# Gated mix of sliding-window attention and a gated feed-forward network: the last 1024 tokens' down projection as seven products of block sums, transposed

## The chip, the core and the metric

The kernel runs on one core of a Trainium2 chip, in one launch. Its engines are PE (TensorE, matrix products into PSUM), DVE (VectorE), ACT (ScalarE), POOL (GpSimd) and SP (SyncE, which issues most DMAs). Each engine works through its own instructions in order; they wait for each other by semaphores. The metric is the device time of one execution in microseconds (us).

## The reference

```python
x = A_x                                        # 2048 tokens x 512
g = sigmoid((x * gate_w).sum(-1, keepdims=True))
q, k, v = heads(x @ wqkv)                      # 32 heads of 16
s = q @ k.T * 16 ** -0.5                       # key i - 255 .. i for query i
a = (softmax(s) @ v) @ wo
b = (silu(x @ w_gate) * (x @ w_up)) @ w_down   # 512 -> 1792 -> 512
return g * a + (1 - g) * b
```

All of it is fp32.

## The kernel before, in words

**Precision.** An fp32 product is made of three matmuls on operands that are split into a high part (a cast to fp32r, on ACT) and a low part (a subtraction, on DVE or POOL): high x high, high x low, low x high. `split` makes the parts (lines 67 and 70), `mm3` issues the three matmuls (L85 to L87). A matmul has 128 rows of depth and 512 moving columns; 12 of them make one *step* of a down projection: one hidden tile of 128 rows, one chunk of 512 tokens, four blocks of 128 tokens.

**Tiles.** The 2048 tokens are four chunks (c = 0 to 3) of 512; the 1792 hidden columns are 14 tiles of 128; the 32 heads are eight groups of four.

**First part, to 598 us.** After a start of about 85 us (values, first projections) come eight groups of 16 slots. A slot (some 4.1 us) is written out by hand in program order: for each of its four heads two score products (L275, L314), their maximum (DVE, L277) and exponential (ACT, L316), three pairs of matmuls of a *lane* (L225: the gate and up products of the hidden tiles 0 to 12 and the q/k projections, into PSUM buffers `pa` and `pb`), and whatever the table `AT` holds for this slot and head (`later(t, hd, f)`). Once in four slots `av` (L338) multiplies the exponentials with the values, and `finish` (L353 to L368) takes its result out of PSUM in five pieces: a copy on ACT, an addition and a copy on DVE (L355, L357), a transpose, the division, a transpose back and the store to `od`. The gate and up products go to DRAM (`raws`, L525). Waiting weights are fetched one ahead into one buffer `raw` (L75), whose low half POOL makes. Before a group begins, its q and k rows are copied into place by SP (`stack`, L258 and L259) out of a pair of buffers `xhi`, `xlo` (`x_pair`). In the last slots `tile0` (L588, L589) makes the hidden tile 0 of chunk 0 and its two halves `TILE0`.

**Tail, from 598 us.** For each chunk 14 steps. Hidden tile `ORDER[n]` is loaded from `raws` (L689, two loads of 256 KB into the pool `got`, four buffers each), goes through SiLU (ACT, L703) and a product (DVE, L704), is split (L67, L70) and is multiplied with the split down weights (`step`). Tile 13 (the second of `ORDER`) has its gate and up products made here, 24 matmuls a chunk (L700). The attention's output projection (`attn_out`, 12 matmuls for each of the 16 token blocks) lies between the steps of chunks 1 to 3. The two results are weighted and added (`put`, L675), and `out` is stored in blocks of 128 tokens. `last_steps` does the last two steps block by block, so that each block's end (L745) runs beside the next block's matmuls; its last block's last step is done in two halves of 256 columns.

## Time and profile before

| | us |
|---|---|
| median of 3 runs (lowest, highest) | 821.86 (821.36, 822.3) |
| span of the profiled execution | 821.5 |
| DVE busy | 515.6 |
| ACT busy | 448.9 |
| POOL busy | 351.8 |

The page lists no time of the profiled execution beside its span, so the span stands for it. A row of a timeline reads: start, length, engine, line, operation, output from inputs, shape, count, and in brackets the idle time ahead of it with what ended it. A row of the windows has busy time and instruction count of PE, PE's weight loads, DVE, ACT and POOL, then clock, DMA share and GB/s. The clock granted to TensorE is 1.000 over the span, and 133.26 MB are moved by DMA.

### The profile page before, as it was taken

To read this page: it belongs to the slowest core of one execution; us is meant where nothing else is said; L and a number is where in the kernel's file an instruction comes from. 1 tells how busy PE (TensorE), PEld (TensorE's weight loads), DVE (VectorE), ACT (ScalarE), POOL (GpSimd) and SP (SyncE) were. 2 spreads that over 40 slices of the span, in tenths; PEclk is the share of its full clock that TensorE was granted. 3 is DMA by queue.
4 is the path that set the end of the run, shared out by engine and by line. 5 is a ranking of instruction groups with operands and counts; after the bars stand their busy time and mean duration, and the time that the engine had idled before them with its cause. 6 is when DMAs were issued, how large, how long until landed. Compare 5 with 4: busy or idle time off the path is not lost.

```text
span 821.5 us, 21573 instructions
## 1 busy us (share of the span) xinstructions
PE 815.1 (99%) x8329; PEld 683.8 (83%) x8329; DVE 515.6 (63%) x1437; ACT 448.9 (55%) x936; POOL 351.8 (43%) x640
## 2 busy tenths in 40 slices
PE   8999999999999999999999999999999999999998
PEld 7888988888888888888888888888887888888886
DVE  6397677677667676677677667756567453443543
ACT  6422666666656666666666666656654433333341
POOL 7812555555546555645554655456511221011020
PEclk9999999999999999999999999999999999999999
DMA  8574534624534543552562463466698563383531
GB/s 294 164 206 150 154 121 125 191 94 146 166 128 125 161 146 117 152 170 101 144 193 102 126 191 125 160 207 201 210 325 267 182 197 110 131 244 107 178 125 51
DMA packets 67957, 133.26 MB, mean 162 GB/s; under 512 B 11600, under 2 KB 16336, under 8 KB 67856
## 3 DMA queue, kind: packets, MB, share of 16 engines
q1 hardware_dynamic: 63888, 118.00, 46.3%
q0 software_dynamic: 3968, 13.90, 4.6%
q8 instruction: 65, 1.06, 0.6%
q14 instruction: 36, 0.29, 0.1%
HBM read 61.08 MB, written 45.61 MB: 130 GB/s over the span
## 4 chain that ended last, share of the span: by engine, by line
PE 95%; DMA 2%; DVE 1%; ACT 1%; issue 1%; SPq 0%; DVEq 0%; ACTq 0%
PE pb L225 24%; PE pa L225 24%; PE pb L338 7%; PE ps L275 6%; PE ps L87 5%; PE ps L85 5%; PE ps L86 5%; PE ps L314 5%; PE pb L205 2%; PE pa L205 2%; PE pb L85 2%; PE pb L87 2%; PE pb L86 2%; PE ps L338 2%; DMA got<-raws 1%; PE pb L700 1%
## 5 line engine op out<-in xcount | busy, mean ns | idle before, releaser
L277 DVE CUSTOM_DVE_ANT_0 ps<-ps,mask 128x384 f32<-128x384 f32 (+2 forms) x512 | 271.6, 539 | 143.2 <-PE ps L314 66.7
L316 ACT ACTIVATE pt<-ps 128x384 f32<-128x384 f32 (+2 forms) x512 | 240.7, 477 | 114.9 <-PE ps L275 57.7
L318 POOL TENSOR_SCALAR_AFFINE_SELECT pt<-pt 128x256 f32<-128x256 f32 x256 | 107.4, 419 | 223.8 <-ACT pt L316 220.4
L314 PE MATMUL ps<-q,k 64*128 64x384 f32 (+2 forms) x512 | 159.9, 329 | 0.0
L275 PE MATMUL ps<-k,q 63*128 63x384 f32 (+2 forms) x512 | 158.7, 330 | 0.0
L225 PE MATMUL pb<-xhi,wh 64*128 64x512 f32 x512 | 111.3, 394 | 0.0
L225 PE MATMUL pb<-xlo,wh 64*128 64x512 f32 x512 | 110.1, 391 | 0.0
L225 PE MATMUL pb<-xhi,wl 64*128 64x512 f32 x512 | 109.9, 392 | 0.0
L225 PE MATMUL pa<-xhi,wh 64*128 64x512 f32 x512 | 109.0, 394 | 0.0
L225 PE MATMUL pa<-xhi,wl 64*128 64x512 f32 x512 | 107.9, 391 | 0.0
L225 PE MATMUL pa<-xlo,wh 64*128 64x512 f32 x512 | 107.8, 391 | 0.0
L275 PEld LDWEIGHTS ps<-k,q 63*128 63x128 f32 x512 | 88.8, 185 | 16.9 <-issue 5.7
L321 POOL TENSOR_SCALAR_AFFINE_SELECT pt<-pt 128x256 f32<-128x256 f32 x224 | 98.7, 441 | 0.0
L314 PEld LDWEIGHTS ps<-q,k 64*128 64x128 f32 x512 | 89.9, 184 | 5.4 <-issue 0.8
L704 DVE TENSOR_TENSOR sg<-got,sg 128x512 f32<-128x512 f32 x51 | 45.1, 885 | 64.6 <-ACT sg L703 59.9
L338 PE MATMUL ps<-pt,vg 64*32 64x320 f32 (+4 forms) x1408 | 75.0, 346 | 0.0
L338 PE MATMUL pb<-pt,vg 64*32 64x320 f32 (+3 forms) x1360 | 73.9, 350 | 0.0
L277 DVE DVE_READ_ACCUMULATOR2_ANT mx<- 128x1 f32 x512 | 71.9, 140 | 0.0
L338 PEld LDWEIGHTS pb<-pt,vg 64*32 64x32 f32 x1360 | 46.4, 106 | 28.3 <-ACT pt L316 9.9
L225 PEld LDWEIGHTS pb<-xhi,wh 64*128 64x128 f32 x512 | 56.6, 185 | 7.9 <-ACT ev L522 0.3
L225 PEld LDWEIGHTS pb<-xhi,wl 64*128 64x128 f32 x512 | 56.5, 184 | 6.7
L225 PEld LDWEIGHTS pa<-xhi,wl 64*128 64x128 f32 x512 | 54.7, 184 | 7.4
(159 smaller groups left out, 1576.6 us busy)
## 6 DMA issues: line engine op xcount, KB each, us to landing
raws<-ev SPq DMA_DIRECT2D x104, 256.0 KB
got<-raws SPq DMA_DIRECT2D x102, 256.0 KB
od<-o POOLq DMA_DIRECT2D x32, 256.0 KB, 2.6
raw<-wgu SPq DMA_DIRECT2D x28, 256.0 KB
q<-xhi SPq DMA_DIRECT2D x56, 128.0 KB
k<-xhi SPq DMA_DIRECT2D x56, 128.0 KB
vd<-vs POOLq DMA_DIRECT2D x8, 672.0 KB, 5.1
vg<-vd SPq DMA_DIRECT2D x32, 168.0 KB
```

The lines of the kernel that those rows point to most:

```text
L85: nc.tensor.matmul(ps, lh, rh, start=start and i == 0, stop=False, skip_group_check=skip)
L86: nc.tensor.matmul(ps, lh, rl, start=False, stop=False, skip_group_check=skip)
L87: nc.tensor.matmul(ps, ll, rh, start=False, stop=stop and i == n - 1, skip_group_check=skip)
L225: mm = nc.tensor.matmul(ps[me], w[r], x[r], start=not second and i == 0, stop=bool(second) and i == n - 1)
L275: nc.tensor.matmul(ps[:, :n], QT[g % 2][pr][r, q0:q0 + P], KT[g % 2][pr][r, k0:k0 + n], start=True, stop=True)
L277: mx = nc.vector.tensor_tensor_reduce(out=ps[:, :n], in0=ps[:, :n], in1=mask[:, 3 * P - n:], scale=1.0, scalar=NEG, op0=ALU.add, op1=ALU.m ...
L314: nc.tensor.matmul(ps[:, :n], KT[g % 2][pr][r, k0:k0 + P], QT[g % 2][pr][r, k0:k0 + n], start=True, stop=True)
L316: BEHIND.append(nc.scalar.activation(pt[:, j, :n], ps[:, :n], AF.Exp, scale=SCALE))
L318: nc.gpsimd.affine_select(out=pt[:, :, :P], in_=pt[:, :, :P], pattern=[[0, 2], [1, P]], compare_op=ALU.is_ge, fill=0.0, base=0, channel_mu ...
L321: nc.gpsimd.affine_select(out=pt[:, :, 2 * P:], in_=pt[:, :, 2 * P:], pattern=[[0, 2], [-1, P]], compare_op=ALU.is_ge, fill=0.0, base=-1, ...
L338: nc.tensor.matmul(AV[g, c][h][32 * j:32 * j + 32, q0 - c * CH:q1 - c * CH], VG[4 * g + kb // 4][o, kb % 4, 17 * j:17 * j + 32], PT[g, kb, ...
L704: nc.vector.tensor_tensor(out=sg, in0=gu[1], in1=sg, op=ALU.mult)
```

## The change

Let H be the hidden activations of the last 1024 tokens, cut into 2 x 2 blocks: tokens of chunk 2 or 3, hidden tiles 0 to 6 or 7 to 13. The down weights are cut into 2 x 2 blocks as well: tiles 0 to 6 or 7 to 13, output columns 0 to 255 or 256 to 511. The product of two such matrices needs eight block products; with sums and differences of blocks as operands seven do (a scheme of Strassen and Winograd). Each is 7 tiles x 2 column blocks x 3 matmuls. They are made transposed: weights stand still, 512 tokens move.

- *Sums of weights* (`sums`, new): 14 sets, two in each of the first seven groups, each for one pair of weight tiles and half their columns. At slot 16g+3 or 16g+6 two loads of 128 KB into `xhi`; one slot later, at head 2, four additions of 128x128 on DVE (L593); one more slot later a split, and two stores of 256 KB to `sd`.
- *`raws`* keeps gate and up of a tile and chunk side by side, so that one load of 512 KB takes both. `ORDER` pairs tile k with tile k + 7.
- *Gates* of chunks 2 and 3 go to DRAM and come back spread over all partitions, since in a transposed result the gate varies along the columns.
- *Tail, first part:* the step of `TILE0` comes first, then the last tile's products of all four chunks (`last_tile`, 96 matmuls), then the remaining steps of chunks 0 and 1, with the attention output of these chunks as 8 steps among them ("a"), then the attention output of chunks 2 and 3, transposed, as 8 steps ("T"). Beside them the 26 loaded activations of chunks 2 and 3 are made (`ready`) and held, and their block sums formed (`first_sum`, `third_sum`, `operand`). `got` has four buffers of 512 KB, which all of these share with the stored weight sums.
- *Tail, last part:* 49 steps of 6 matmuls in the order of products 1, 5, 6, 2, 7, 3, 4 (`block`), with the operands three steps ahead (`LEAD`); the results of a product are put together and weighted by `after` and `finished`, two pieces a step, and stored to a second output `outT`.
- The tail's splits are by ACT and DVE; POOL has none.

The core of the diff:

```diff
-    raws = dram.tile([NF - 1, 2, NCH, P, CH], F32, name="raws")
+    raws = dram.tile([NF - 1, NCH, P, 2, CH], F32, name="raws")
+    sd = dram.tile([4, P, NP, 2, HD], F32, name="sd")
-    ORDER = [0, NF - 1, *range(1, NF - 1)]
+    ORDER = [0, NF - 1, 7, 1, 8, 2, 9, 3, 10, 4, 11, 5, 12, 6]
...
+        def sums(t, k, d):
+            u = slice(d * P, d * P + P)
+            buf = []
+            def load():
+                buf.extend(x_pair())
+                uv = buf[0][:, :CH].bitcast(F32).rearrange("p (r c) -> p r c", c=P)
+                for m in range(2):
+                    nc.sync.dma_start(uv[:, 2 * m:2 * m + 2], wd[k + NP * m].rearrange("p (r c) -> p r c", r=2)[:, :, u])
+            def add():
+                parts = buf[0].bitcast(F32).rearrange("p (r c) -> p r c", c=P)
+                a11, a21, a12, a22, *to = (parts[:, r] for r in range(8))
+                for n, (x, y, op) in enumerate(((a21, a22, ALU.add), (to[0], a11, ALU.subtract),
+                                                (a11, a21, ALU.subtract), (a12, to[1], ALU.subtract))):
+                    nc.vector.tensor_tensor(out=to[n], in0=x, in1=y, op=op)
...
+            later(t, 1, load)
+            later(t + 1, 2, add)
+            later(t + 2, 0, halve)
+            later(t + 2, 3, store)
+        for m in range(2 * NP):
+            sums(m // 2 * NB + 3 + m % 2 * 3, *divmod(m, 2))
...
-        hp = B.enter_context(tc.tile_pool(name="hp", bufs=3, side="right"))
+        hp = B.enter_context(tc.tile_pool(name="hp", bufs=4, side="right"))
...
+        HALF["h", 0, 0] = TILE0
+        multiply(("h", 0, 0))
+        source(plan[0][0])
+        last_tile(0)
...
+        last_tile(3)
+        gates()
...
+        def operand(p, k):
+            if p == 6:
+                sub(T1[k], R[k + NP, 3], T1[k])
+            if p == 4:
+                sub(T1[k], R[k + NP, 2], T1[k])
...
+        def block(p, k, ds=range(2), cols=slice(0, CH)):
+            hh, hl = HALF[p, k]
+            for d in ds:
+                mm3(bank(p)[d][:, cols], [(block_weights(p, k, d), (hh[:, cols], hl[:, cols]))],
+                    start=p in (1, 5, 2, 3) and k == 0, stop=k == NP - 1, skip=True)
...
+        x = BANK["pa"]
+        for d in range(2):
+            for cols in ((slice(0, CH),), (slice(0, CH // 2), slice(CH // 2, CH)))[d]:
+                for p, k in steps[end:]:
+                    block(p, k, (d,), cols)
+                for f in finished(2, 2 + d, x[d], cols=cols):
+                    f()
```

The lines of the changed kernel are 4 higher than those of before in the attention part (L277 is L281, L225 is L229, L355 is L359, L357 is L361), and 2 higher in `split` and `mm3` (L70 is L72, L85 to L87 are L87 to L89).

**Order on DVE in an attention slot.** DVE in slot 16g+4 at head 2, where `finish` takes a result out of PSUM. An ISA row pair is a score block's maximum; `o` is the result, `pb` the PSUM buffer. Before:

```order
L277 ISA ps_8680,mx<-ps_8680,mask 128x384
L277 ISA mx 128x1
L355 TENSOR_TENSOR o_1341<-pb,o_1341 128x448
L357 COPY o_1341<-pb 128x64
L277 ISA ps_8698,mx<-ps_8698,mask 128x384
```

The changed kernel:

```order
L281 ISA ps_8830,mx<-ps_8830,mask 128x384
L281 ISA mx 128x1
L593 TENSOR_TENSOR xhi<-xhi 128x128 x4
L359 TENSOR_TENSOR o_1347<-pb,o_1347 128x448
L361 COPY o_1347<-pb 128x64
L281 ISA ps_8852,mx<-ps_8852,mask 128x384
```

The four additions stand between the maximum and the pair that empties `pb`.

**Order on PE at the start of the tail.** The last value product (L338, now L342) and what follows it. Before:

```order
L338 MATMUL ps_10569<-pt,vg 32x128
L700 MATMUL pa<-xhi_71,wh 128x512
L700 MATMUL pa<-xlo_72,wh 128x512
L700 MATMUL pa<-xhi_71,wl 128x512
```

The changed kernel (`k_363` holds TILE0's halves, `q_90` the down weights):

```order
L342 MATMUL ps_10745<-pt,vg 32x128
L87 MATMUL ps_10837<-q_90,k_363 128x512
L88 MATMUL ps_10837<-q_90,k_363 128x512
L89 MATMUL ps_10837<-q_90,k_363 128x512
L87 MATMUL ps_10838<-q_90,k_363 128x512
```

The 12 matmuls of the first step moved ahead of the last tile's gate and up products.

**Order on PE and DVE at the end.** PE's last step and a half, in the changed kernel, with the engines that a row waits for; `pa` is the last result (128 output columns by 512 tokens, halves of 256):

```order
L89 MATMUL pa<-hh,k_362 128x256
L87 MATMUL pa<-hh,q_90 128x256
L88 MATMUL pa<-hl,q_90 128x256
L89 MATMUL pa<-hh,q_90 128x256
L87 MATMUL pa<-hh,q_361 128x256 [waits DVE_49]
L88 MATMUL pa<-hl,q_361 128x256
```

And DVE's last rows there (L72 is a low half, L835 a difference of operands, L963, L966, L969 the addition, gate product and last addition of a result):

```order
L835 TENSOR_TENSOR xhi_11480<-h_10976,xhi_11480 128x512
L72 TENSOR_TENSOR hl<-xhi_11480,hh 128x512
L963 TENSOR_TENSOR sg<-ps_12453,woh 128x512
L966 TENSOR_TENSOR sg<-sg,xlo_11016 128x512
L72 TENSOR_TENSOR hl<-xhi_11480,hh 128x512
L969 TENSOR_TENSOR sg<-sg,raw_12026 128x512
L963 TENSOR_TENSOR sg<-ps_12454,woh 128x512
L966 TENSOR_TENSOR sg<-sg,xlo_11016 128x512
L969 TENSOR_TENSOR sg<-sg,raw_12027 128x512
L966 TENSOR_TENSOR sg<-pa,xlo_11016 128x512
L969 TENSOR_TENSOR sg<-sg,k_11949 128x512
L966 TENSOR_TENSOR sg<-pa,xlo_11016 128x256
```

Where before four results followed their matmuls one by one at the end, the last operand's low half now stands among the results of another product, and PE's last nine matmuls stand behind the gate product of the first half of their own PSUM tile.

401 lines of the change are left out of this document (285 added, 116 removed).

## The prediction

> **What bounds the kernel now.** I read the page first, its busy times and its chain, then the waits of the matmul engine, then the timeline at the places that the change touches.
>
> ```profile
> span 821.5 us, 21573 instructions
> PE 815.1 (99%) x8329; PEld 683.8 (83%) x8329; DVE 515.6 (63%) x1437; ACT 448.9 (55%) x936; POOL 351.8 (43%) x640
> PE 95%; DMA 2%; DVE 1%; ACT 1%; issue 1%; SPq 0%; DVEq 0%; ACTq 0%
> ...
> PE pa L180 <- POOL ident masks.py:199: 1.4, 1, 1.4
> PE ps L87 <- DVE hl L70: 0.4, 1, 0.4
> ```
>
> PE (TensorE's matmuls) is busy 99% of the span and makes 95% of the chain, and its list of waits (last two rows: microseconds in total, times, longest) is nearly empty. So each matmul removed pays its full pace, and each wait that appears on PE costs its full length: no idle time on PE is left to take it. The first thing needed is that pace, from the chain:
>
> ```profile
> 640.86 2.72 PE pa L700 x12
> 643.58 2.72 PE pb L700 x12
> ```
>
> Twelve matmuls of 512 columns take 2.72 us, 0.2267 us each.
>
> **The removed matmuls: -9.5 us.** The down projection of chunks 2 and 3 was 2 x 14 steps of 12 matmuls, 336. It becomes 7 products x 7 tiles x 6, 294. The attention output of these chunks is only transposed and keeps its count, and so does the last gate/up tile. 42 x 0.2267 = 9.52 us. The rows of PE fall from 6758 to 6722 in the order, 36 and not 42, because nine matmuls, not three, now stand as two halves (6 more rows, 0.07 us). The rest of this part asks where PE must now wait.
>
> **The first step of the tail: +2.9 us.** The tail began with 24 gate/up products (L700) that need nothing new. Now chunk 0's first down step (operand TILE0) stands there.
>
> ```profile
> 598.11 1.28 ACT L588 ACT_TABLE_LOAD   x1
> 599.40 0.63 ACT L588 ACTIVATE ev<-k 128x512 f32<-128x512 f32 x1
> 600.07 0.69 DVE L589 TENSOR_TENSOR ev<-k,ev 128x512 f32<-128x512 f32 x1 [4.59 <-ACT ev L588]
> 600.79 0.62 ACT L67 CAST k<-ev 128x512 fp32r<-128x512 f32 x1 [0.76 <-DVE ev L589]
> 601.45 0.69 DVE L70 TENSOR_TENSOR k<-ev,k 128x512 fp32r<-128x512 f32 x1 [0.69 <-ACT k L67]
> 598.87 0.50 PE L700 MATMUL pa<-xhi,wh 128*128 128x512 f32 x1
> ...
> 604.22 0.39 PE L700 MATMUL pb<-xhi,wl 128*128 128x512 f32 x1
> ```
>
> The five rows of ACT (ScalarE) and DVE (VectorE) are one dependent chain that the change leaves alone. It ends at 601.45 + 0.69 = 602.14. PE is free at 598.87; the step's first two matmuls need the cast (601.41), the third the subtraction. It starts near 602.2 where it could have stood at 598.87 + 0.45: 2.9 us, formerly covered by the L700 products. I see no cover now; bounds 2.5 to 3.2.
>
> **The sums in the attention slots: +4.5 us.** 14 times, two DMA loads, four DVE additions of 128x128, a cast, a subtraction and two stores are put into the slots, some 0.9 + 0.6 us of DVE each. DVE has 37% of its time free, so only the place counts. The additions stand in order (first excerpt above) ahead of the L355/L357 pair that empties a PSUM buffer. In the group of 355 us:
>
> ```profile
> 359.06 0.57 DVE L277 CUSTOM_DVE_ANT_0 ps<-ps,mask 128x384 f32<-128x384 f32 x1 [2.33 <-PE ps L314]
> 359.55 0.14 DVE L277 DVE_READ_ACCUMULATOR2_ANT mx<- 128x1 f32 x1
> 359.55 0.62 DVE L355 TENSOR_TENSOR o<-pb,o 128x448 f32<-128x448 f32 x1
> 360.08 0.22 DVE L357 COPY o<-pb 128x64 f32<-128x64 f32 x1
> 360.21 0.56 DVE L277 CUSTOM_DVE_ANT_0 ps<-ps,mask 128x384 f32<-128x384 f32 x1
> 360.43 0.33 PE L314 MATMUL ps<-q,k 64*128 64x384 f32 x1
> ...
> 360.60 0.41 PE L225 MATMUL pb<-xhi,wh 64*128 64x512 f32 x2
> 98.92 0.21 DVE L357 COPY o<-pb 128x64 f32<-128x64 f32 x1
> 99.14 0.55 PE L225 MATMUL pb<-xhi,wh 64*128 64x512 f32 x2
> ```
>
> The L225 product on `pb` takes the buffer that L357 empties at 360.30, so it has 0.30 us to spare; in the first group (98.92 + 0.21 against 99.14) it has none. From 64 columns to 448 the start-to-start time of such operations goes from 0.13 to 0.53 us in these rows (360.08 to 360.21, 359.55 to 360.08), which gives about 0.20 us for 128; with two dependent hand-overs the four take about 0.9 us. PE then waits 0.9 - 0.3 = 0.6 us in six groups and 0.9 in the first: 4.5 us. No row shows a 128x128 addition. The lower bound is 0.5 us (the next L277 can slip and PE reaches `pb` later than shown); the upper is four durations of 0.29, the 128-column row of L277 below, or 1.16 us, giving 6 x 0.86 + 1.16 = 6.3.
>
> ```profile
> L277 DVE CUSTOM_DVE_ANT_0 ps<-ps,mask 128x128 f32<-128x128 f32 x32 | 9.2, 294 | 32.8 <-PE ps L275 24.4 <-POOL x10lo L70 6.1 <-PE ps L314 2.3
> ```
>
> The Trainium skill, "VectorE: DVE Perf Modes", section on the TRN2 errata, puts an fp32 tensor_tensor at (N+151)/0.96 ns and says that small tiles pay the fixed part each time; for 512 it gives 0.69, as L589 above shows. By it an addition is 0.29 us, and four in a row would make the upper 6.3 us; the overlap of consecutive rows above (0.62 long, the next 0.53 later) speaks for less. The second set of a group stands three slots later, by the same rows at a place with no pair to empty: 0 to 0.1 us each, in the bounds.
>
> The additions also wait for their loads, and DVE works in order: a late load holds all behind it.
>
> ```profile
> 350.85 0.60 SPq L259 DMA_DIRECT2D k<-xhi  x1
> ...
> 353.71 1.13 SPq L525 DMA_DIRECT2D raws<-ev  x2
> 362.76 0.33 SPq L75 DMA_DIRECT2D raw<-wgu  x1
> 370.19 0.14 DVE L277 DVE_READ_ACCUMULATOR2_ANT mx<- 128x1 f32 x1
> od<-o POOLq DMA_DIRECT2D x32, 256.0 KB, 2.6
> ```
>
> SP (the queue that issues) reaches the first pair of loads after 353.71, behind the last copy out of the same buffer (issued 350.85). With 1 us of issue and the 2.6 us of the only 256 KB transfer that the page times, it lands near 358.6, before 359.55. The second pair comes behind the wait that ends at 362.76, five issues of about 0.5 us and its own slot, and lands near 369; the additions follow the row of 370.19 there. Both are close, and the same SP also carries the attention's own loads.
>
> **The tail's loads: +1.5 us.** The first of them must wait for all stores of the attention output, the last of which is issued at 605.28:
>
> ```profile
> 605.28 0.56 POOL L368 DMA_DIRECT2D od<-o  x1 [5.83 <-DVE o L367]
> ```
>
> With 2.6 us to land and 3 to load, data come near 612. The 96 products of the last tile, 21.8 us, now stand ahead of the first step that needs them and hide this. Then loads of 512 KB replace pairs of 256 KB, and the tiles of chunks 2 and 3 come earlier: while the remaining steps of chunks 0 and 1 run, 20 steps or 54.4 us ask for 35 loads and 1 MB of stores or other loads, 19.4 MB, 357 GB/s. What such loads got:
>
> ```profile
> 600.00:610.00 10.00, 10.00 (x46) 8.28 (x45) 7.45 (x13) 5.49 (x11) 0.56 (x1) 1.00 0.95 333
> 610.00:620.00 10.00, 10.00 (x46) 8.29 (x45) 9.76 (x18) 2.98 (x5) 0.00 (x0) 1.00 0.92 313
> 620.00:630.00 10.00, 9.64 (x42) 7.40 (x41) 7.71 (x10) 5.81 (x10) 2.78 (x2) 1.00 0.89 292
> ```
>
> (Last columns: clock, DMA share, GB/s.) At 333 the 19.4 MB take 58.3 us, 3.9 too many, which three spare buffers of the four (1.5 MB, 4.7 us) about cover. At 292 they take 66.4 us, 12 too many, 7 uncovered. I take 1.5, near the best row, since the 292 was not asked for more; bounds 0 and 7. The Trainium skill, "DMA: Bandwidth & Descriptors", section Specifications, states about 358 GB/s of HBM per core; by it the stage would just fit and this term would be 0. The rows stay below that at a share of 0.95, so the measured rates decide.
>
> **The end: +5.0 us.** Before, four L745 operations follow their matmuls on an idle DVE:
>
> ```profile
> 817.40 0.28 PE L87 MATMUL ps<-k,hl 128*128 128x256 f32 x1
> 817.72 0.88 DVE L745 SCALAR_TENSOR_TENSOR k<-ps,igate,k 128x256 f32<-128x256 f32 x2 [0.64 <-PE ps L87]
> ```
>
> Last matmul to end of span is 821.5 - 817.68 = 3.8 us, 2.9 of it behind DVE (818.60). Now each operand of the last product is a subtraction, a cast and a subtraction, and DVE also does the results of products 7 and 3. From the first operand of product 4 to the last low half stand 21 DVE operations in order, 21 x 0.60 (512 columns by the two start-to-start times above), with hand-overs between dependent ones and the last cast about 14.0 us. PE needs it at 8 steps x 1.36 + 8 x 0.2267 = 12.7: **1.3 late**. Behind that half DVE still has four operations of product 3, two of product 4's first column block, and the first 256-wide one, about 4.4 us; and the matmuls of the last 256 columns wait for that one (third excerpt), where they could have followed after 1.5: **3.0**. After them stand a multiplication and an addition in place of one operation, 0.44 more, and some 0.3 of hand-over: **0.7**. The 3.0 is order alone; if the operands are in time the sum is 3. If DVE runs as in this row (885 ns against 600), it reaches 8.
>
> ```profile
> L704 DVE TENSOR_TENSOR sg<-got,sg 128x512 f32<-128x512 f32 x51 | 45.1, 885 | 64.6 <-ACT sg L703 59.9 <-DMA got<-raws 4.7
> ```
>
> **Sum.** 821.5 - 9.5 + 2.9 + 4.5 + 1.5 + 5.0 = 825.9 in the profiled execution, which lies 0.4 below the median of the runs (821.86): **826**.
>
> **Rivals.**
> - *The additions fit and the loads come in time.* DVE's free 37% speaks for it, the in-order rows above against. Attention 0.5, loads 0, end 3.0: 821.5 - 9.5 + 2.9 + 0.5 + 3.0 = 818.4, with the median 818.7, faster.
> - *One of the two large terms fails.* Attention hidden, the end as computed: 821.5 - 9.5 + 2.9 + 0.5 + 1.5 + 5.0 = 821.9, with the median 822.2, no difference.
> - *The loads bound the middle of the tail*, as soon as they get under about 310 GB/s over those 54 us; the rows of 313 and 292 speak for it, that these were not asked for more against it. 7 in place of 1.5: 831.7, slower.
> - *The second pair of loads in each group is late* by 0.7 us, which holds DVE and then PE in six groups: +4.2, about 830.4. This decides as soon as the landing passes 370.2.
> - That the matmuls do not go away is excluded by the order; what can fail is only that PE uses the time.
>
> **How the numbers follow.** A measurement of this kernel tells 0.2% (1.6 us) from no change, so faster is under 820.2 and slower over 823.5. The forecast has 0.46 (0.06 of it in its lower flank, within 0.2%), the first rival 0.29, the second 0.09, the loads 0.10, the late pair 0.06. Faster 0.29, same 0.06 + 0.09 = 0.15, slower 0.40 + 0.10 + 0.06 = 0.56. The range leaves out the far halves of the first rival and of the load-bound case: 817 to 832. The forecast's own range is 823 to 829.
>
> **What would show it.** Right: a wait of PE of 2 to 3 us just before its first down step at 599; waits of 0.6 on `pb` behind the copy of the attention pair, seven times; two gaps on PE in its last 20 us, the larger ahead of its last nine matmuls; under 1.5 us of waits in between. Wrong: no PE wait on DVE in the attention slots (the first rival), additions that idle for their DMA (the late pair), or a row of PE waits in steps 12 to 31 that end with DMA (loads). The prediction fails as a whole if PE's listed waits add up to under 8 us.

## The result, and the profile after

| | before | changed |
|---|---|---|
| median of the runs beside each other (lowest, highest), us | 822.08 (821.36, 823.23) | 851.16 (850.42, 854.79) |
| span of the profiled execution, us | 821.5 | 849.8 |
| granted clock over the span | 1.000 | 0.987 |

The changed kernel is slower: ratio 1.036, 95% interval 1.0336 to 1.0384. The prediction was 826.0 (817 to 832). The sign was right and the size was not. In the experiments below one run of `r_end`, 899.05 us at a granted clock of 0.85, is left out as slow.

The head of the changed kernel's page (busy times, the granted clock in 40 slices, the chain by engine):

```profile
span 849.8 us, 21755 instructions
PE 822.3 (97%) x8293; PEld 687.4 (81%) x8293; DVE 579.2 (68%) x1598; ACT 472.1 (56%) x973; POOL 325.9 (38%) x621
PEclk9999999999999989999999999999999999999998
PE 72%; DMA 14%; DVE 6%; issue 3%; SPq 3%; ACT 2%; POOL 1%; DVEq 0%; ACTq 0%; POOLq 0%
```

What PE waited for in it (total us, times, longest):

```profile
PE pb L229 <- DVE o L361: 6.8, 7, 2.7
PE ps L87 <- ACT k L780: 3.4, 1, 3.4
PE pa L89 <- DVE hl L72: 2.7, 1, 2.7
PE ps L87 <- ACT k L69: 2.6, 1, 2.6
PE pa L87 <- DVE sg L966: 2.5, 1, 2.5
PE pa L87 <- ACT hh L69: 1.9, 2, 1.3
...
PE pa L88 <- DVE hl L72: 1.0, 1, 1.0
```

PE's list of waits was nearly empty before and now holds over 20 us. PE is still 97% busy, and that number misleads twice. Its busy time rose by 7 us with 36 matmuls fewer, largely because some of them ran at a lower clock (0.50 for 22 us of the span in all). And the chain, which was PE for 95%, is now PE for 72%: at places DMA (14%) and DVE (6%) set the time.

To see where the time went, the starts of the matmuls are compared. In the first part the score products (L275, now L279) stand at the same count in both kernels, so the difference of their starts is what was lost so far. In the tail each matmul of 512 columns should start 0.2267 us after the one ahead; what exceeds that is a loss. All in us, from the two profiled executions (the drain is the time from the last matmul to the end of the span):

| term | predicted | measured |
|---|---|---|
| 42 matmuls removed | -9.5 | -9.5 (by count: 927 matmuls in the tail for 963, 18 of them of 256 columns for 6) |
| sums in the attention slots | +4.5 | **+15.0** |
| first step of the tail | +2.9 | +2.6, and 0.9 in the rest of the first 108 matmuls |
| the tail's loads (middle of the tail) | +1.5 | **+14.6** |
| the end (last 100 matmuls, and the drain) | +5.0 | +5.4, and 0.1 in the drain |
| before's own small losses in the tail | - | -1.0 |
| sum | +4.4 | +28.1 (the spans differ by 28.3) |

**The attention slots.** The first set of sums of a group (timelines of DVE, PE and POOL at 370 us), at first as the prediction drew it:

```profile
369.70 1.02 DVE L593 TENSOR_TENSOR xhi<-xhi 128x128 f32<-128x128 f32 x4
370.63 0.62 DVE L359 TENSOR_TENSOR o<-pb,o 128x448 f32<-128x448 f32 x1
...
371.44 0.50 PE L229 MATMUL pb<-xhi,wh 64*128 64x512 f32 x1 [0.28 <-DVE o L361]
...
371.58 1.30 POOL L72 TENSOR_TENSOR wl<-raw,wh 128x512 fp32r<-128x512 f32 x1
372.29 1.14 DVE L72 TENSOR_TENSOR xlo<-xhi,xlo 128x512 fp32r<-128x512 f32 x1
```

The four additions take 0.93 us (369.70 to 370.63; estimated 0.9), and PE waits for `pb`. But the low half of the sums, at head 0 of the next slot, starts at 372.29 and takes 1.14 us in place of 0.69 beside a POOL operation of the same kind. It holds the maxima back, and score products wait for those. This group lost 0.8 between the score products of 369.7 and 372.2 us, at the pair, 1.0 up to that of 375.1, which stands behind the low half, and 0.35 after that, the second set among it. By group the loss is 1.2, 1.4, 1.7, **6.2**, 1.4, 1.4 and 2.1 (15.4, less 0.4 at the start), the second sets 0.1 to 0.4 of each. The fourth group, at 299 us:

```profile
299.26 2.38 DVE L593 TENSOR_TENSOR xhi<-xhi 128x128 f32<-128x128 f32 x4 [0.97 <-DMA xhi<-wd]
300.20 1.29 POOL L72 TENSOR_TENSOR wl<-raw,wh 128x512 fp32r<-128x512 f32 x1
301.56 0.61 DVE L359 TENSOR_TENSOR o<-pb,o 128x448 f32<-128x448 f32 x1
...
302.36 0.79 PE L229 MATMUL pb<-xhi,wh 64*128 64x512 f32 x1 [2.75 <-DVE o L361]
```

The loads are 0.97 us late, the four additions then take 2.30 us (299.26 to 301.56), the last of them beside POOL's operation, and PE stands 2.75 us. What comes next is seen only in the windows (us from the span's start; length; busy time and count of PE, its weight loads, DVE, ACT, POOL; clock, DMA share, GB/s):

```profile
296.00:298.00 2.00, 2.00 (x64) 1.45 (x47) 0.33 (x1) 0.62 (x2) 0.14 (x1) 1.00 1.03 351
...
302.00:304.00 2.00, 1.64 (x8) 1.45 (x10) 1.90 (x7) 0.29 (x1) 0.00 (x0) 0.50 0.66 161
...
306.00:308.00 2.00, 2.00 (x12) 1.72 (x12) 0.74 (x3) 0.86 (x2) 0.00 (x0) 0.50 1.04 305
```

For six microseconds behind the wait the granted clock is 0.50: the wait is paid a second time. The first row shows the loads' surroundings: DMA ran at 351 GB/s at a share of 1.03 just before they landed, full of what SP had issued ahead of them. Over the seven groups the additions waited for their loads three times, 1.8 us in all.

This loss changes from execution to execution. Ten traces here have the attention part of the changed kernel, and they lost 10.5 to 19.9 us in it. What does not change is a group whose loads are in time: 1.2 to 1.5 us each. In the trace of run 10 below six groups lost 1.2 to 1.4 and the fourth, with loads 2.0 us late and the clock at 0.50 behind the wait, 6.7.

**The middle of the tail.** Windows again, the last row over 100 us:

```profile
650.00:660.00 10.00, 10.00 (x45) 8.26 (x44) 6.77 (x11) 6.30 (x11) 0.00 (x0) 1.00 0.99 355
...
670.00:680.00 10.00, 7.40 (x33) 5.80 (x31) 5.56 (x10) 4.55 (x8) 0.00 (x0) 1.00 0.86 260
680.00:690.00 10.00, 9.24 (x34) 7.54 (x35) 6.59 (x11) 5.89 (x11) 0.00 (x0) 0.83 0.73 243
...
710.00:720.00 10.00, 5.94 (x25) 4.28 (x25) 6.48 (x11) 3.54 (x8) 0.00 (x0) 0.91 0.78 245
720.00:730.00 10.00, 10.00 (x34) 8.07 (x35) 5.03 (x8) 2.87 (x6) 0.00 (x0) 0.75 0.83 292
645.00:745.00 100.00, 91.77 (x379) 72.95 (x379) 62.70 (x98) 48.27 (x84) 0.00 (x0) 0.95 0.83 279
```

The row of 720 has a PE that is 100% busy, and 34 matmuls where other rows have 45: busy time says nothing there, count and clock do. How a late load becomes a wait of PE is seen on the timeline of ACT and PE at 677 us:

```profile
677.06 0.63 ACT L729 ACTIVATE xhi<-got 128x512 f32<-128x512 f32 x1 [2.97 <-DMA got<-raws]
678.34 0.63 ACT L729 ACTIVATE sg<-got 128x512 f32<-128x512 f32 x1 [0.65 <-DMA got<-raws]
678.88 0.60 ACT L69 CAST hh<-got 128x512 fp32r<-128x512 f32 x1
679.50 0.63 ACT L729 ACTIVATE xhi<-got 128x512 f32<-128x512 f32 x1
680.04 2.40 ACT L780 ACTIVATE k<-ps,igate 128x512 f32<-128x512 f32 x4
680.76 0.80 PE L87 MATMUL ps<-q,hh 128*128 128x512 f32 x1 [3.36 <-ACT k L780]
```

PE lists ACT's L780, which empties PSUM, as the one it waits for. But L780 stood in ACT's order behind three activations and a cast, and the first activation had waited 2.97 us for a hidden tile that was not needed yet. The list of what ended ACT's idle time ahead of L729 (us, times) gives the sum of such waits:

```profile
  DMA got<-raws: 56.0, 33
```

ACT stood 56 us at tiles, 10.1 of it at the first one of the tail, and only a part of it reached PE. The middle's 14.6 us are four waits of PE (3.36, 1.32, 2.73 and 0.55, together 8.0), 16 matmuls at half clock (0.43 us each in place of 0.2267: 3.3) and smaller waits.

**The end.** The changed kernel's last matmuls and DVE's last rows:

```profile
839.58 0.51 PE L88 MATMUL pa<-hl,q 128*128 128x512 f32 x1 [0.96 <-DVE hl L72]
843.43 0.42 DVE L966 TENSOR_TENSOR sg<-pa,xlo 128x256 f32<-128x256 f32 x1
843.90 0.39 PE L87 MATMUL pa<-hh,q 128*128 128x256 f32 x1 [2.50 <-DVE sg L966]
845.83 0.42 DVE L966 TENSOR_TENSOR sg<-pa,xlo 128x256 f32<-128x256 f32 x1 [1.52 <-PE pa L89]
```

The two waits are there, 0.96 and 2.50 (predicted 1.3 and 3.0). The rest of the 5.4 is 0.7 at two smaller waits ahead of them, at 824 and 833 us, and mostly half clock behind them.

### The profile page after: what moved, and what is told of

The parts are those of the page before. It is cut to its first block, busy times and chain, and to the rows that moved or that the text cites. A ratio compares the mean times of both kernels' runs of the same rounds, so it can differ in the third digit from the quotient of the medians.

```text
span 849.8 us, 21755 instructions
## 1 busy us (share of the span) xinstructions
PE 822.3 (97%) x8293; PEld 687.4 (81%) x8293; DVE 579.2 (68%) x1598; ACT 472.1 (56%) x973; POOL 325.9 (38%) x621
## 4 chain that ended last, share of the span: by engine, by line
PE 72%; DMA 14%; DVE 6%; issue 3%; SPq 3%; ACT 2%; POOL 1%; DVEq 0%; ACTq 0%; POOLq 0%
PE pb L229 22%; PE pa L229 20%; DMA got<-raws 8%; PE pb L342 6%; PE ps L279 5%; PE ps L318 4%; PE pb L209 2%; DMA xhi<-wd 2%; DMA raws<-ev 2%; PE pa L89 1%; PE pa L87 1%; PE pa L88 1%; PE ps L87 1%; PE ps L89 1%; PE ps L342 1%
## 5 line engine op out<-in xcount | busy, mean ns | idle before, releaser
L281 DVE CUSTOM_DVE_ANT_0 ps<-ps,mask 128x384 f32<-128x384 f32 (+2 forms) x512 | 270.6, 538 | 135.3 <-PE ps L279 74.3
L279 PE MATMUL ps<-k,q 63*128 63x384 f32 (+2 forms) x512 | 161.1, 335 | 0.0
L229 PE MATMUL pb<-xhi,wh 64*128 64x512 f32 x512 | 121.3, 399 | 6.8 <-DVE o L361 6.8
L229 PE MATMUL pb<-xlo,wh 64*128 64x512 f32 x512 | 119.3, 397 | 0.0
L229 PE MATMUL pb<-xhi,wl 64*128 64x512 f32 x512 | 118.4, 395 | 0.0
L229 PE MATMUL pa<-xhi,wh 64*128 64x512 f32 x512 | 112.4, 394 | 0.0
L229 PE MATMUL pa<-xhi,wl 64*128 64x512 f32 x512 | 111.4, 391 | 0.0
L229 PE MATMUL pa<-xlo,wh 64*128 64x512 f32 x512 | 111.2, 391 | 0.0
L279 PEld LDWEIGHTS ps<-k,q 63*128 63x128 f32 x512 | 89.5, 186 | 19.8 <-issue 5.7
L229 PEld LDWEIGHTS pb<-xhi,wh 64*128 64x128 f32 x512 | 63.6, 187 | 15.5 <-DVE o L361 9.4
L342 PE MATMUL ps<-pt,vg 64*32 64x320 f32 (+4 forms) x1408 | 75.0, 346 | 0.0
L342 PE MATMUL pb<-pt,vg 64*32 64x320 f32 (+3 forms) x1360 | 74.0, 351 | 0.0
L281 DVE DVE_READ_ACCUMULATOR2_ANT mx<- 128x1 f32 x512 | 71.5, 140 | 0.0
L342 PEld LDWEIGHTS pb<-pt,vg 64*32 64x32 f32 x1360 | 46.5, 106 | 28.1 <-ACT pt L320 6.9
L229 PEld LDWEIGHTS pb<-xhi,wl 64*128 64x128 f32 x512 | 63.8, 187 | 5.8
L229 PEld LDWEIGHTS pb<-xlo,wh 64*128 64x128 f32 x512 | 63.2, 188 | 0.2
L229 PEld LDWEIGHTS pa<-xhi,wl 64*128 64x128 f32 x512 | 57.8, 184 | 6.5
```

What stands on the lines that cost most here:

```text
L229: mm = nc.tensor.matmul(ps[me], w[r], x[r], start=not second and i == 0, stop=bool(second) and i == n - 1)
L279: nc.tensor.matmul(ps[:, :n], QT[g % 2][pr][r, q0:q0 + P], KT[g % 2][pr][r, k0:k0 + n], start=True, stop=True)
L281: mx = nc.vector.tensor_tensor_reduce(out=ps[:, :n], in0=ps[:, :n], in1=mask[:, 3 * P - n:], scale=1.0, scalar=NEG, op0=ALU.add, op1=ALU.m ...
L342: nc.tensor.matmul(AV[g, c][h][32 * j:32 * j + 32, q0 - c * CH:q1 - c * CH], VG[4 * g + kb // 4][o, kb % 4, 17 * j:17 * j + 32], PT[g, kb, ...
```

## The experiments

The whole times of these kernels scatter by several microseconds with the clock's drops, so beside the ratio each run is read by the losses of its stages, worked out as in the table above. "Attention", "start" (wait and the rest of the first 108 matmuls), "middle", "products", "end" (last 100 matmuls) and "drain" (last matmul to end of span) are, for the changed kernel, 15.0, 2.6 + 0.9, 14.6, 0, 5.4 and 4.0. (The expectations still reckon with 4.7 for the end, and 8.7 with the drain; by this measure it is 9.4.) A stage that an edit leaves alone scatters too: the attention over ten traces from 10.5 to 19.9, the middle over seven from 12.3 to 14.9, end and drain over nine from 8.9 to 9.8. Only what lies outside is put down to an edit.

**1. Move TILE0's step behind the last tile's first products** (`r_tile0`).

```diff
         HALF["h", 0, 0] = TILE0
-        multiply(("h", 0, 0))
         source(plan[0][0])
         last_tile(0)
+        multiply(("h", 0, 0))
```

> The changed kernel with one step put back: the last tile's 24 gate and up products of chunk 0 come first on TensorE, the step of TILE0 after them. Theory: the wait of 2.6 us (and 0.45 us for the low half) ahead of the first step of the tail goes, 2.9 us, so about 848.2 in place of 851.2. Rival: the loads that follow later bind the tail, and what is won at 614 us is waited for again between 670 and 740: 850.5 or more, with the waits there longer by the same amount.

848.36 us, ratio 1.0324 (1.0296 to 1.0352). In the profiled execution the wait of 2.6 is gone and the tail is no shorter (236.2 us from the last value product to the end of the span, 236.1 in the changed kernel): start 2.8, middle 16.0. PE now waits for ACT's L745, which stands behind casts of late down weights, and longer at the loads' place (L780). From its list of waits:

```profile
PE ps L87 <- ACT k L780: 4.4, 1, 4.4
...
PE pa L742 <- ACT h L745: 1.8, 1, 1.8
```

In this trace the term was a real wait but not an additive one: what binds next is the loads. It is of the longest of the four executions (852.53), though; the median is what the expectation said, and its interval overlaps that of the changed kernel. Whether the whole gains is therefore open. With the loads spread as well (`r_m4` to `r_m7`) the start lost 0.1.

**2. Sums on POOL** (`r_sums_pool`), and **3. the same, with the split a slot later** (`r_sums_late`).

```diff
-                    nc.vector.tensor_tensor(out=to[n], in0=x, in1=y, op=op)
+                    nc.gpsimd.tensor_tensor(out=to[n], in0=x, in1=y, op=op)
...
-                split(buf[1][:, :CH], ..., nc.scalar, nc.vector)
+                split(buf[1][:, :CH], ..., nc.scalar, nc.gpsimd)
... (3 only)
-            later(t + 2, 0, halve)
-            later(t + 2, 3, store)
+            later(t + 3, 0, halve)
+            later(t + 3, 3, store)
```

> The changed kernel with the four additions and the low half of each set of weight sums made by GpSimd in place of VectorE; every DMA of the sums stays. Theory: VectorE's strict order is what costs in the attention slots (its additions stand ahead of the pair that empties PSUM and wait for their loads); the attention then loses under 4 us against the kernel before, in place of 15, and the time is 838 to 840. Rival: the sums' DMA traffic and SyncE's issues delay the attention's own loads; then at least 10 us of the 15 stay and the time is 846 or more.

> The changed kernel with the additions and the low half of the weight sums on GpSimd, as in the run before, and the cast and the stores of each set one slot later. Theory: with the additions on GpSimd what was left of the loss (11 of 15 us in that run) came from ScalarE, which stood in order at the cast of a sum that was not there yet; with the cast a slot later the attention loses under 4 us against the kernel before (its last value product at 598.6 us, with 15 lost at 613.7). Rival: the DMA traffic of the sums and SyncE's issues cost it; then 8 us or more stay lost.

Run 2: 849.67, ratio 1.0325 (1.0291 to 1.0358), attention 11.1, inside the scatter of the ten. The waits on `pb` behind DVE are gone and another stands in their place. The cast of the sums now waits in ACT's order for POOL's additions and holds what ACT does next (list of PE's waits):

```profile
PE pb L342 <- ACT ev L526: 8.9, 7, 1.7
```

Run 3: **839.31**, ratio 1.0203 (1.0182 to 1.0224), attention **1.4**, and no wait of PE in the slots. The same additions take longer (0.46 us for 0.29), wait longer for their loads, and hold nobody (one line's instructions: duration min/median/max in ns; then what it waited for):

```profile
L593 POOL TENSOR_TENSOR xhi<-xhi x56: 452/463/476, 96.2 to 504.1; 128x128 f32<-128x128 f32 x56
...
  DMA xhi<-wd: 8.7, 5
```

So all of the loss but 1.4, at least 9 us of it, came from where the sums stood in the order of DVE and ACT, not from their loads, stores and additions as such.

**4. The last 18 matmuls ahead of the operations that finish the first half** (`r_end`).

```diff
-            for cols in ((slice(0, CH),), (slice(0, CH // 2), slice(CH // 2, CH)))[d]:
+            parts = ((slice(0, CH),), (slice(0, CH // 2), slice(CH // 2, CH)))[d]
+            for cols in parts:
                 for p, k in steps[end:]:
                     block(p, k, (d,), cols)
+            for cols in parts:
                 for f in finished(2, 2 + d, x[d], cols=cols):
```

> The changed kernel with the last 18 matmuls of 256 columns all put ahead of the operations that finish the two halves. Theory: the wait of 2.5 us ahead of the last nine matmuls goes and with it the half clock behind it; VectorE's chain then sets the end and gives 1.3 to 2 us: about 849.5. Rival: VectorE's own chain of finishing operations sets the end already, and moving the matmuls gives under 0.4 us.

845.63, ratio 1.03 (1.0243 to 1.0358). End 2.2 and drain 5.7, together 7.9 for 9.4, a gain of 1.5 as expected: of the 3.2 won ahead of the last matmul 1.7 came back as drain, because DVE has the same work left.

**5. and 6. The end's other operations on POOL**: the gate product and last addition of the results of products 2, 7 and 3 on POOL, added to run 4 (`r_end_pool`), then also each half's results into a tile of its own (`r_end_fix`).

```diff
             def mult():
-                nc.vector.tensor_tensor(out=t, ...
+                eng = nc.vector if other is None else nc.gpsimd
+                eng.tensor_tensor(out=t, ...
```

> The changed kernel with the last 18 matmuls ahead of the finishing operations, and the gate product and last addition of products 2, 7 and 3 on GpSimd, which has nothing to do there. Theory: the in-order queue of VectorE makes the loss of 4.7 us at the end (1.3 us for late low halves, the rest behind the results of product 3); then the last 100 matmuls lose under 1 us and what follows the last matmul stays at about 4.0 us: 4 us less in the tail. Rival: the operands' own chain (difference, cast, low half) is too slow for three steps of lead; then 1.1 us of waits on the low half stays, and 2 us or more in all.

> The changed kernel with the last 18 matmuls ahead of the finishing operations, the later operations of products 2, 7 and 3 on GpSimd, and buffers of their own for the last two results. Theory: in the run before, the last results waited 1.6 and 1.8 us for the stores of the two buffers they took over; with that gone, end and drain together (8.7 us in the changed kernel, 11.5 in that run) come to 6.5 or less. Rival: GpSimd, at 1.3 us an operation, is the last to finish; 8 us or more.

Both came out longer, not shorter: 850.84, ratio 1.0351 (1.031 to 1.0392), end and drain 11.5; 852.2, ratio 1.0376 (1.0355 to 1.0396), end and drain 10.3. The timeline of run 6 shows one reason: a DVE operation that takes 0.69 us elsewhere takes 1.50 beside POOL's.

```profile
838.19 1.28 POOL L971 TENSOR_TENSOR sg<-sg,raw 128x512 f32<-128x512 f32 x1
838.52 1.50 DVE L971 TENSOR_TENSOR h<-h,k 128x512 f32<-128x512 f32 x1
```

**7. DVE's order at the end** (`r_end2`): run 4, the differences for product 4 made during products 2 and 7, and the results of product 3 taken two steps sooner.

```diff
-            if p == 4:
-                sub(T1[k], R[k + NP, 2], T1[k])
...
+            if 23 <= s < 23 + NP:
+                sub(T1[s - 23], R[s - 23 + NP, 2], T1[s - 23])
...
-                jobs += [(s + LEAD, f) for f in after(p)]
+                jobs += [(s + (1 if p == 3 else LEAD), f) for f in after(p)]
```

> The changed kernel with the last 18 matmuls together, the seven differences that product 4 needs made during products 2 and 7, and the results of product 3 taken two steps sooner. Theory: the order of VectorE sets the end; with seven operations out of its last ten steps and none of product 3 behind the last low half, the last 100 matmuls lose 0.5 us or less and 4.0 to 4.7 us follow the last matmul, 4 us less than the 8.7 us of the changed kernel. Rival: the end is bound by something else in the chain from difference to cast to low half; 7 us or more of the 8.7 stay.

848.17, ratio 1.0302 (1.0284 to 1.032). End **0.5** and drain 4.8, together 5.3 for 9.4, with no operation less. On DVE's timeline the last low half is done at 841.98, and PE's matmul that needs it starts at 842.03:

```profile
841.29 0.69 DVE L72 TENSOR_TENSOR hl<-xhi,hh 128x512 fp32r<-128x512 f32 x1
842.80 0.69 DVE L964 TENSOR_TENSOR sg<-pa,xlo 128x512 f32<-128x512 f32 x1 [0.82 <-PE pa L89]
```

Behind it DVE waits for PE, no longer PE for DVE. The attention lost 19.9 in this execution, the longest of the four (851.36), so the gain does not show in its whole time.

**8. Cheaper loads of the attention output** (`r_od_rows`: whole rows of the same size, which leaves out the choice of the right rows, so the result is another), and **9. the same data stored without the unread rows** (`r_od_compact`, four stores for one, each load contiguous by rows).

```diff
 (8)
-                    heads = od[2 * (n + m):2 * (n + m) + 2].rearrange("g (j e) s -> (g j) e s", e=32)
-                    nc.sync.dma_start(raw[:, m], heads[:, :DH, c * CH:(c + 1) * CH])
+                    nc.sync.dma_start(raw[:, m], od[n + m, :, c * CH:(c + 1) * CH])
 (9)
-            nc.gpsimd.dma_start(od[g, :, c * CH:(c + 1) * CH], both)
+            for j in range(4):
+                nc.gpsimd.dma_start(od[g, DH * j:DH * j + DH, c * CH:(c + 1) * CH], both[32 * j:32 * j + DH])
```

> The changed kernel with the 16 loads of attention results in the tail (256 KB each, gathered from 16 of each 32 rows) replaced by loads of whole rows of the same size; the attention output projection is therefore fed other data. Theory 1: these loads take 1.2 to 1.9 us each where other data of the size take 0.7, and this holds up the loads behind them; the waits of TensorE between 650 and 745 us fall from 14.6 to 8 us or less, 843 to 845. Theory 2: the four buffers, each held until its tile is used, set the pace, whatever a single load takes: at least 12 of the 14.6 us stay, 849 or more.

> The changed kernel with the attention results stored to DRAM without the 16 of each 32 rows that nobody reads, in four stores each from GpSimd, so that the tail's 16 loads of them read whole rows; the result stays the reference's. Theory: as with the rows of other data, the middle of the tail loses about 9.5 us in place of 14.6, and GpSimd's extra issues cost the attention under 1 us. Rival: the extra issues delay the masks behind them, and the attention loses 3 us more.

848.11, ratio 1.0322 (1.0299 to 1.0344), middle 9.5; 848.75, ratio 1.0311 (1.028 to 1.0344), middle 11.4. In the changed kernel these 256 KB landed 1.1 to 2.2 us after the transfer ahead of them when queued, the 512 KB of a hidden tile mostly 1.2 to 1.5: about half the rate. Against the scatter of 12.3 to 14.9 that is worth 3 to 5 us of the middle in run 8 and 1 to 3.5 in run 9, not all of it.

**10. Half of the bytes of the 26 loaded tiles** (`r_half`: only the gate half is loaded and serves as both factors, so the result is another).

```diff
-            if kind in "hr":
+            if kind == "r":
+                nc.sync.dma_start(raw[:, 0], raws[n, c, :, 0])
+            elif kind == "h":
                 nc.sync.dma_start(raw, raws[n, c])
```

> The changed kernel with only the gate half of each of the 26 tiles of chunks 2 and 3 loaded, 256 KB in place of 512, and used for both factors; the output of those chunks is therefore another. Count, order and buffers of the loads stay. Theory 1, bytes: the stretch then asks for some 230 GB/s, under the 245 to 355 that it got, and the 14.6 us of waits in the middle fall to 6 or less. Theory 2, buffers and latency: a load takes about 3 us from issue to its first bytes whatever its size, and four buffers allow so many loads in a time; then 11 us or more stay.

841.83, ratio 1.022 (1.0153 to 1.0287), middle **5.5** for 14.6:

```profile
645.00:745.00 100.00, 97.32 (x419) 79.07 (x418) 67.19 (x106) 51.34 (x90) 0.00 (x0) 0.98 0.71 234
```

Instructions, buffers and order are the same; 419 matmuls in place of 379 start in these 100 us (same window as above). Of the middle's loss 7 to 9 us went with the bytes: for the most part it is bound by what is moved.

**11. The first loads sooner** (`r_got_first`: the pool `got` made ahead of `hp`, so that its buffers lie where older ones come free).

```diff
-        hp = B.enter_context(tc.tile_pool(name="hp", bufs=4, side="right"))
         got = B.enter_context(tc.tile_pool(name="got", bufs=4, side="right"))
+        hp = B.enter_context(tc.tile_pool(name="hp", bufs=4, side="right"))
```

> The changed kernel with the buffers of the tail's loads placed in memory ahead of the operand buffers, so that they lie in space that is free when the attention ends and the first load no longer waits for the last stores of the attention results (first data came 13.2 us after the last value product, at 626.9 us against 613.7). Theory 1: this late start sets the middle of the tail back; with data some 8 us earlier the waits of 14.6 us fall to 8 or less. Theory 2: the stretch itself asks for more than the loads give, and four tiles of head start change little: 12 us or more stay.

851.96, ratio 1.0359 (1.0323 to 1.0394), middle 13.9. Data come some 8 us sooner, four buffers are full and wait, and the middle is inside its scatter.

**12. Loads spread over more of the tail** (`r_early`): eight of the 26 made beside the last tile, the other 18 at even distances over 32 steps, the late down weights ahead of them in the queue, with run 1's edit.

```diff
-        at = [*range(1, 12, 2), *range(12, 12 + 22)]
-        at = at[:len(todo)]
+        first, todo = todo[:8], todo[8:]
+        at = [1 + i * 32 // len(todo) for i in range(len(todo))]
...
+        for f, c in first[:3]:
+            ready(f, c)
```

> The changed kernel with eight of the 26 activations of chunks 2 and 3 loaded and made beside the last tile's products, the other 18 spread evenly over the following 33 steps, the late down weights fetched ahead of them, and the TILE0 step behind the last tile's first products. Theory: the waits of 14.6 us in the middle of the tail come of a demand of about 290 to 360 GB/s in one stretch while the DMA engines stand nearly idle in the 30 us ahead of it; with the demand spread the middle loses under 5 us and the tail (last value product to the end, 236 us) takes 224 or less. Rival: each wait is one slow gather of attention results or a buffer that is held, whatever the demand; at least 10 of the 14.6 us stay.

846.08, ratio 1.0288 (1.0248 to 1.0328), middle 14.0. The stalls at 680 and 720 are mostly gone (1.0 is left on L780), and one of 8.5 us took their place at 650, PE on ACT's cast of an operand: the eight loads stand in the queue ahead of the first that a step needs.

**13. to 18. Mended versions.** `r_m1` is runs 3, 12 and 5 together; `r_m3` adds runs 6, 9 and 11, with five tiles beside the last tile. `r_m4` has run 3, run 11, run 4, run 1, and the loads spread: five beside the last tile, 15 over 40 steps, six among the products, with the block sums that need those six formed later. `r_m5` is `r_m4` with run 9. `r_m6` and `r_m7` are `r_m4` with run 7 and fewer tiles beside the last tile (three and four), and move the loads of the output weights: one per step in `r_m6`, four steps ahead of their casts in `r_m7`, which also puts the first hidden tile ahead of the down weights in the queue. The core of `r_m7` that none above shows, against the changed kernel:

```diff
-        for _ in range(4):
+        load(*LOADS.pop(0))
+        late = [load_late(m) for m in range(8, 11)]
+        for _ in range(3):
             load(*LOADS.pop(0))
-        late = [load_late(m) for m in range(8, 11)]
...
-        late = [load_wo(k) for k in range(NK)]
+        late = []
...
+            if 1 <= n < 1 + NK:
+                late.append(load_wo(n - 1))
+            if 5 <= n < 5 + NK:
+                late.pop(0)()
...
+            if s % 2 and 5 <= s < 16:
+                ready(*most_late[s // 2 - 2])
```

> Sums on GpSimd with the cast a slot later; buffers of the loads in memory that is free at the end of the attention; five activations early, fifteen spread over the next 40 steps and six among the first two of the seven products, where only sums of weights are loaded; the TILE0 step moved; the last 18 matmuls together. Theory, demand: steps of 2.72 us then ask for 1.4 loads in place of 2, some 265 GB/s, and the middle loses 5 us or less: 822 - 9.5 + 1.4 (attention) + 0.5 + 5 + 4 (end) = 823 to 825. If it is the gathers or the four buffers, 10 us or more stay in the middle and the time is 829 or more.

> r_m6 with the loads of wo issued four steps ahead of their casts, the first activation's load ahead of the late down weights, four activations early, and the late activations behind the first loads of weight sums. Theory: the middle then loses 4 us or less and the products 1; with 2 us in the attention and 0.5 + 0.8 at the end that is 822.2 - 9.5 + 8.3 = 821, no difference from the kernel before, or faster by up to 0.4% if the middle loses nothing. Rival: the four buffers and the gathers keep 7 us or more in the middle; 825 or more, slower.

| | us | ratio (95%) | attention | start | middle | products | end + drain |
|---|---|---|---|---|---|---|---|
| `r_m1` | 838.67 | 1.0203 (1.018, 1.0227) | 1.4 | 0.3 | 19.3 | 0 | 11.5 |
| `r_m3` | 836.80 | 1.0177 (1.0161, 1.0193) | 3.8 | 1.0 | 14.2 | 0 | 10.3 |
| `r_m4` | 828.75 | 1.0085 (1.0065, 1.0105) | 2.2 | 0.1 | 6.7 | 1.8 | 7.9 |
| `r_m5` | 828.96 | 1.0087 (1.007, 1.0104) | 3.6 | 0.1 | 6.1 | 4.2 | 7.9 |
| `r_m6` | 829.51 | 1.0085 (1.007, 1.01) | 2.0 | 0.1 | 10.7 | 2.9 | 5.3 |
| `r_m7` | **826.16** | 1.0053 (1.0035, 1.0072) | 1.1 | 0.1 | 5.4 | 4.7 | 6.0 |

`r_m1`, `r_m3` and `r_m6` had been expected at 821 to 824, 819 to 821 and 818 us and came out slower; `r_m5` was expected within 1 us of `r_m4`, as it came. `r_m7` takes back 25 of the 29 us and stays 0.5% behind the kernel before. Its waits show what is left:

```profile
PE ps L87 <- ACT hh L69: 2.5, 1, 2.5
PE pb L87 <- DMA got<-sd: 2.0, 2, 1.7
PE ps L87 <- ACT k L780: 1.9, 1, 1.9
PE pa L87 <- DMA got<-sd: 1.5, 1, 1.5
```

All four go back to loads through `got`: ACT had stood 4.5 and 3.4 us at a tile ahead of the first and third, and the tiles moved to the products delay the stored weight sums there. The sum closes: losses of 1.1 + 0.1 + 5.4 + 4.7, and 2.2 at the end beyond before's drain of 3.8, are 13.5; less the 9.5 of matmuls and before's own 1.0 that is 3.0, and the spans are 824.5 and 821.5.

## Why the prediction failed

- **The removed matmuls, -9.5: right**, by their count.
- **The sums in the attention slots, +4.5: the first step that failed** (15.0, and 10.5 to 19.9 over ten traces, above its upper bound of 6.3). The additions were as worked out (0.93 us for 0.9), and what was lost at the pair nearly so (0.8 in a group whose loads were in time, for 0.6); a second set lost 0.1 to 0.4, for 0 to 0.1. Three things were not in the sum. The split of the sums, "some 0.6 us of DVE" whose place "only counts", was given no place and no price; it holds the maxima a slot later. The loads of the **first** set were late, which the text put 0.95 us in time from one group, while the rival of late loads was given the second set. And a wait was priced at its own length, though it can halve the clock behind it. Run 3 shows that the place in two queues decides: 1.4 with the same loads, stores and additions; run 2, which also puts them on POOL but leaves ACT's cast where it was, moves the wait to ACT and wins nothing clear. How the loss divides among the three was not tried one by one. Seven groups at the 1.2 to 1.5 us of a group in time would make some 9 us (an estimate), twice the term; late loads and the clock behind them are then the rest, which is what changes between executions.
- **The first step, +2.9: right as a wait** (2.6), with one thing missed: in the one trace without it (run 1) the tail was no shorter, since the loads' lateness stood behind it.
- **The tail's loads, +1.5: the second step that failed** (14.6, and 12.3 to 14.9 over seven traces, above its upper bound of 7). The rate taken was near the best row, 333 GB/s; it was 243 to 292 in the rows from 670 on. The three spare buffers were counted as cover, but ACT takes the tiles in order, and a late tile holds the emptying of PSUM behind it. The rival "the loads bound the middle" was the right mechanism at half its size. Runs 8, 9 and 10 show it: halving the tiles' bytes takes 7 to 9 us out of the middle, contiguous loads of the attention output 3 to 5 or 1 to 3.5. Run 11 shows that the start of the loads is not it, run 12 that eight tiles ahead only move the stall; `r_m4`, which spreads the loads into the products and has run 11's edit, lost 8.5 in the middle and the products together.
- **The end, +5.0: right** (5.5), in its mechanism, DVE's order, and in part by luck in its size: the two waits were a little shorter than worked out, the drain grew by 0.1 in place of 0.7, and two smaller waits and the half clock, which were not in the sum, made up for it. Run 4 alone won 1.5 of the 3.0 that "order alone" should give, because the other work of DVE then stood at the very end; with that moved (run 7) end and drain come to 5.3, 1.5 above the 3.8 of before.
- Of the signs that it named, the wait ahead of the first step, the seven waits on `pb` and the two gaps at the end came; the fourth, under 1.5 us of waits in between, did not. The waits of the middle, which it would have known by DMA, stand in PE's list under ACT.
- The estimate of the first rival, that it all fits (818.7), is out of reach even of run 3's attention, run 7's end and half the bytes at once, which no run had together: with 1.4, 3.5 at the start, 5.5 and 1.5, and 9.5 and 1.0 off, the span would be 822.9 (an estimate).

What stays open: how the rest of the middle's loss divides between the pattern of the transfers, the latency of a load behind four buffers, and the drops of the clock. That the windows at 670, 680 and 710 got 243 to 260 GB/s at a DMA share of 0.73 to 0.86, while that at 650 got 355 at 0.99, comes at least in part of SP not issuing. A tile's issue takes SP 0.3 us, and here are its timelines of the changed kernel at 664 and 706 us:

```profile
670.12 11.13 SPq L710 DMA_DIRECT2D got<-raws  x6
706.85 9.01 SPq L710 DMA_DIRECT2D got<-raws  x4
```

It issued no load from 674.7 to 678.4 us and none from 711.1 to 715.5. Its waits ahead of L710 end mostly with DVE's product (L730, 24.3 us in 20 waits for `sg` alone), which frees a buffer and itself waits for ACT at the late tile: a late load delays the issue of the next ones.

## What to carry to other kernels

Where one engine is 99% busy, work given to its helpers is priced by where it stands in their queues and by how late its own data may come, not by its length: the same sums cost 10.5 to 19.9 us in DVE's order, 11.1 with the additions moved to POOL and ACT's cast left in place, and 1.4 with the cast a slot later. Take for a stage that will ask for all of the bandwidth not the best rate of the profile but the worst of a mixed one, and ask which engine will stand in order at the late load and whom it serves besides. And a change that trades matmuls for bytes and element-wise passes must find room for both where they fall: here the loads of the tail came late at 279 GB/s, and the last passes stood in DVE's way at the end.

## What the hardware showed beside

- **A wait can halve TensorE's clock, and which one does is not fixed by its length.** The wait at the start of the tail (2.55 or 2.56 us, behind TILE0's cast) stands in ten traces. In four, the changed kernel's among them, the clock stayed at 1.00 behind it; in six it fell to 0.50 for 3.4 us. The windows just behind it, in the changed kernel and in run 10:

```profile
617.00:619.00 2.00, 2.00 (x10) 1.43 (x9) 1.90 (x5) 0.00 (x0) 0.00 (x0) 1.00 0.00 0
```

```profile
616.00:618.00 2.00, 2.00 (x5) 1.55 (x6) 1.93 (x4) 0.21 (x1) 0.00 (x0) 0.50 0.00 0
```

  Over all these traces the shortest single wait with a drop behind it took 1.7 us (run 1, at 734.9), the longest without one 3.2 (`r_m3`, at 676.3), and a drop that ended inside the span lasted 3.4, 6.8 or 10.2 us. The Trainium skill, "TensorE: Matmul & The Clock Gate", Part 1, says that the clock is set by activity in a window of 3413 ns that runs freely, so that where work lies in the window matters. The ten equal waits and the steps of 3.4 us agree with that; its table's condition of one idle window, about 3.4 us, does not, since most drops here followed shorter waits.
- **DVE and POOL slow each other down.** A DVE operation with two inputs in SBUF took 1.50 us for 0.69 (run 6), 1.14 for 0.69 (at 372 us) and, an addition of 128x128 at 300 us, 1.34 for 0.29 beside a POOL operation of the same kind. In these three rows it ended 0.15 to 0.55 us after POOL's operation did, as if it had stood still until then. In run 6 POOL's own operations of that kind took 1.6 to 1.7 us where such a DVE operation was running in their first 0.5 us, and 1.3 in the three other cases. The Trainium skill, "GPSIMD Engine Reference", section Specifications, names this contention without a size; these rows give it one.
